# A linear-attention and mixture-of-experts kernel: its large loads on one queue, its gate products on GpSimd, its last batch's P@V in two groups, and a new order of all tasks

## The chip, the core and the metric

The kernel runs on one NeuronCore of a Trainium2 chip. A core has a matrix engine (TensorE, PE in the rows; its weight loads are a row of their own, PEld), a vector engine (VectorE, DVE), a scalar engine (ScalarE, ACT), a general engine (GpSimd, POOL) and an engine that mostly issues transfers (SyncE, SP). Each engine executes its own instructions in the order in which they were written, and waits for the others by semaphores. The core has 16 DMA engines, which move data between the chip's memory and the core's own memory (SBUF). TensorE writes its products to eight PSUM banks, which the other engines read. Transfers are issued by an engine into that engine's queue; here SyncE and ScalarE issue them.

The metric is the device time of one execution in microseconds (us); less is better. A profiled execution gives, beside its time, a trace of each instruction.

## What is computed

There are 8 batches of 8 heads, 576 tokens, head dimension 64. Each head goes through linear attention without a softmax and a root-mean-square norm; the eight heads side by side are the input `x` (8 x 576 x 512) of a layer of four attention experts, of which each token takes two:

```python
kv = np.einsum('bhsd,bhse->bhde', k, v)
out = np.einsum('bhsd,bhde->bhse', q, kv)
x = out / np.sqrt(np.mean(out * out, axis=-1, keepdims=True) + 1e-06) * g_norm
# x: heads side by side, [B, S, 512]
logits = x @ w_gate                      # [B, S, 4]; the two largest are kept
w = softmax over the two kept logits
for e in range(4):                       # head dimension 64, causal
    a = softmax(causal((x @ wq[e]) @ (x @ wk[e]).T / 8))
    ye = a @ (x @ wv[e]) @ wo[e]
    out[tokens that kept e] += w[:, e] * ye
```

## The kernel before, in words

**Tasks.** The whole program is a list of 1071 tasks that the file holds written out; nothing in the file works it out. `names` gives every task its name, `ORDER` holds two base-64 digits for each place in the list, `ENGINE` one letter for each task (S: SyncE's queue, C: ScalarE's queue, A: ScalarE, V: VectorE, G: GpSimd, F: a matmul over all 128 rows where it is over 64 otherwise), and `SLOTS` says which PSUM bank or which buffer each task takes. The loop at the end of the kernel emits the tasks in this order; since every engine executes in order, the list alone sets what stands ahead of what. The semaphores between engines follow from the data.

**A batch** goes through these tasks, in the kernel's names with the lines of the code before:

- `lk`, `lv`: four transfers each for K and V, by half of the heads and by one of two runs of tokens (256 or 320 KB). K and V have two buffers each, and `SLOTS` says which one a batch takes; a load waits until `kv` has read what its buffer held before.
- `lq`: three transfers for Q, one of 576 KB over 128 partitions for the even head pairs and two of 288 KB over 64 partitions for the odd ones. Q has two buffers.
- `kv` (L379): K^T V on TensorE, 80 small matmuls. `kvc`, `kvx`: copies from PSUM to `kvs`, and from there with the 32-row blocks swapped to `kvm` (L392 where GpSimd does it; L296 and L297 are the shared lines of copies on ScalarE and VectorE).
- `qc` (L401): Q is turned on VectorE. `o` (L414): Q times kv on TensorE. `oc`, `sq` (L438 where GpSimd does it): copy and square of the result.
- `ms`, `G` (L446): sums of the squares and the gate's products by matmul; then the inverse root with one step of refinement over three engines (`ln`, `rs`, `na`, `nb`, `lo`, and `R`, L485). `bc` (L521): the inverse root is spread over partitions by matmul; `xm` (L528): the product is `x`, transposed.
- `L`, `lt`, `ltc`, `lgc`, `m8` ... `gate`: the gate's logits, the two largest of four and their weights, on small tiles.
- `v` (L580), `kp`, `qp` (L600): projections by the weights, which are scaled by `g_norm` beforehand (`lw` loads 256 KB, `ws`, L361 on ScalarE, scales); copies `vc`, `kpc`, `qpc`.
- for each of two pairs of experts: `sc` (L630) scores, `exp` (L642) on ScalarE, `msk` (L649) the causal mask on GpSimd, `pv` (L661) P times V, whose 65th column holds the sum of P.
- `rc` (L676): the reciprocal of that sum on VectorE. `iv` (L680): its product with the gate, ten numbers for each of 128 partitions, on GpSimd or VectorE. `oc2` (L688): the scaling of P@V, on VectorE, for both experts of a pair at once. `ot` (L700): the result is turned on TensorE, `otc` copies it.
- `y` (L727): the product with `wo`, `yc` its copy into one of nine stage buffers (which the weights use too at the start), `st` the store to memory. Every second batch has one more `y` for the last 64 rows of two batches.

The tasks of a batch are interleaved with those of the batches beside it; around 167 us, for example, TensorE does projections and scores of one batch, y of the one before and K^T V of the next.

**Zero matmuls.** `ZEROS` puts 69 matmuls of zeros ahead of four TensorE tasks of the first batch (43 before its first K^T V). Their results aren't used. Being float32, each is two passes (L762, 138 rows).

**Queues.** ScalarE's queue has two loads each of K and V of batch 0, all six Q loads of batches 0 and 1, three of the six loads of wq, wk and wv, and two of the last stores. All else is on SyncE's. Each queue is issued in order: where a transfer has to wait for its buffer, all behind it on that queue wait too.

Of the kernel before, what the change touches and what calls it, by code (L numbers as in the profile page):

```python
# [25 lines left out]
    ("kv", 0, 0): 43, ("o", 0, 1): 12, ("ms", 0): 9, ("bc", 0, 0, 1): 5,  # L26
# [3 lines left out]
    "0602040801000703050U0V0A0W092U0X0Y2T0f0C0g0a0b0B0c0e2V0Z0i0d2N0n2L2S2h0o0h2i0q2R0D0k2M0m0p2O0r2Q0j0l2P0t0u2g0s"  # L30
    "0v0w0K0O0x0G132W2f2X150y0z112Y2Z2a2d160M12142c2e170+182b2k0L0-0H2r2j4R2n0E1q0I0N2l2p1o0P2s2q2m4X0F1H1p2o101L1M"
    "194T2t1r1R1N1I4Q1S2u2v2w4V1s2x2y2z4S334a2+2-1O4Y0J374Z1P344U1C1t381T1w1Q354b361A1U1x391V1X301Y3A3T1e313V1W3U1Z"
    "1y4c4n4W4d4k6c4e1a321z1b3W4l1c3X8b4f213b3P4i6Y1B6b1D1J6U4j6S3L3Q8Z4g1E6a3c6V4h1F4m3M3B1K6X4o203Y4q1f6Z6T4s1g4p"
    "3C1G4w6n4u3Z1u1v4r3f3s3t0Q3q6W4v3r8X223E6o3D1h4t1d4x3a3N1i4y1-1j4+8e1+1k4-231l3O8Y24506m3y0S3u6d6e3z513v6f6g3+"
    "3F5258258d6p6h3-8c26AZ428g3d3g6l538h3G1m3e8a5AAb6j5C1n6k6i4z595B3w5D543x5E0R0T5F6q6r3H6u6s273J8f6w285Y5O6v6x3R"
    "Ai6y5a5Z3i6t3h6z5U5V6+3K558u5P3S6-8i8r4470718j8k8lAgAf56725b3j5773745G3I8s5H8m5c757G7H5dAh8nAj763k5J2F8p7C5Q3l"
    "8oAd3m5R7D8q3n5v415w2G5S7A7E8t5k2I7F5T5x2J7BAa5y5I8w915e5g8-8v92908z5f773o5h8+7W5i5KAc8x788y435-3p5j5z6393Av60"
    "5+7940CgAw619545Ae645LAu6962467U5W5o7cCk96975l477X4898Cm7aAt7x99Cn687bAk7I7V5n5X7d7y9FEo9L7L9JAl5M9M9K9G7JAmAn"
    "66Ao7e7i7kArEqAp2CCi5mEm7l9AAs7S65677T5p2D5q7f7j5N5r497z9H7K5s4AEn947+Aq9IAyB3B181CoCj4HAx82Az6A4I4NA-B07Y9V9X"
    "4BB49W4K6BCeCl6CA+9Y9B4C7Q6D7Z7MB2El7g4D4O4L7R7h887-9CB57mB7Cz9DB829A2C+B97NBA9EB6A37pEh6E807q6F7o9N5tBBBH9O9f"  # L40
    "2AEp9g9hBC5uA0BI9iBN9dC-CfBDBO7nA17O9eBJ7PChBK7r7s9p9q839n84CpBEA47t7uA89oCqCyA5878AA9CrCs85Ct9v869j9QCvBLBFA6"
    "Cx6G4ECuCwBM9kA79PD18BBG6HD84FD02KD69R89BPD29l8C8DD9EiE-2H6MBQD48EC46N8F9SEkD7BX9bD3ACD59c9ZDA9mF1AAF07v4PEjEg"
    "BS9aAB8G6P8H7wBYDCDDE+C59T4GDEErEsDFEtDGBR6Q6REu6JEvC29tExC3BjEyBkDSBh9s6K9UDQBZDT9u4MAFBfDRBiDMEwBgBaEz2EBrBs"
    "BTDH9rBlBmDODBDPDNF2F6BxDIF4ADF39wBnFAAE9x9y9zC8F72BAGF8AHC9Bo8O9+AI8UFBAJBbCABU8PDJF9AKF5FC9-CC8VCBC6DKCDFEBp"
    "DmBqBcDnFFC7BdDoFGALFDCFDpBVCG6OBe6LFHBwAMBWDwCEDLFICIDUFOBvDxDq8RFPE7DV8SBtDkDuDrFJFKE8FSFUBuDl6IDvFLFVFTAQCH"
    "CJCKARE9CL4JDgDhCMFMFQEAFRByEHEBEIDyDsECANBzFNB+B-DeDiATDtFWDWFq8TAWAOEJAUFoDcDjD+FkFpFrDdEFDfEDFlAXDXEGD-E0Fw"
    "8LDY8IEL8MFX8JGBGCC0FxDzAPC1EEFmCNFuENEMAVCOFnFsFyFzFt8WCSFiFvFYEK8KDZG1CTFZG9GAFjFeG0F-E1DaGFE2GDFfDbE3E4EO8N"
# [62 lines left out]
def kernel(  # L110
# [690 lines left out]
```

## Time and profile before

| | |
|---|---|
| three runs | 221.35, 223.86, 224.46 us; median 223.86 |
| profiled execution | 223.62 us; span of the trace 221.9 |
| mean granted clock of TensorE | 0.97 |
| first K^T V of batch 0 begins | 13.77 us |
| TensorE's busy share | 92% |
| bytes moved | 40.33 MB, mean 182 GB/s |

The span is the time from the first to the last instruction of the trace, and what the execution takes beyond it is 1.7 us. A row of a timeline gives the start in us, the duration in us, the engine, the line of the code, the operation, the tile written and the tiles read, their shapes, the number of instructions that were drawn together, and in square brackets for how long the engine had been idle before and what ended the idle time. A row of a group gives the busy time in us and the mean duration of one in ns behind the first bar, and the idle time before them by what ended it behind the second. A row of a line gives the least, middle and longest duration in ns, and the stretch of time in which they lie. A row of the transfers gives the size of one in KB and the middle time in us from issue to landing.

### The profile page before, as it was taken

The page shows a single profiled execution, that of the slowest core. Times are in us where ns is not written, and L with a number is a line of the kernel's source. Part 1 is how long each engine was busy: PE and PEld are TensorE (multiplying, and loading weights), DVE is VectorE, ACT ScalarE, POOL GpSimd, SP SyncE. Part 2 cuts the span into 40 slices and gives each one's busy share as a digit, 9 for nine tenths or more (in the row PEclk, how much of TensorE's full clock was granted, in tenths as well). Part 3 has the DMA queues.
Part 4 walks back from the last instruction along what each step waited for, and adds up shares of the span by engine and source line. Part 5 has one row for each costly group of instructions (what it writes and reads, how often), then busy time and mean ns, then how long its engine had stood idle before and what let it go on. Part 6 is the DMA issues. An engine that isn't in the chain of part 4 may idle for free.

```text
span 221.9 us, 7348 instructions
## 1 busy us (share of the span) xinstructions
PE 204.1 (92%) x3082; PEld 170.3 (77%) x3082; DVE 131.5 (59%) x320; ACT 130.4 (59%) x225; POOL 63.4 (29%) x164
## 2 busy tenths in 40 slices
PE   7999798199999899999999999999996999999990
PEld 7987585177877878796897869878965788999970
DVE  6005578018764883997686477468557457454770
ACT  2002802376769674558645886877566585867851
POOL 7001000010157115317340351143357142234300
PEclk9999999769999999999999999999999799999997
DMA  5999999994079999974089369210270001036386
GB/s 177 357 216 296 293 242 315 238 243 85 4 201 352 334 252 268 233 237 159 4 213 268 116 178 358 92 50 0 100 284 3 1 3 47 28 120 233 99 326 246
DMA packets 34385, 40.33 MB, mean 182 GB/s; under 512 B 9008, under 2 KB 25392, under 8 KB 34352
## 3 DMA queue, kind: packets, MB, share of 16 engines
q1 hardware_dynamic: 28736, 34.95, 54.2%
q10 hardware_dynamic: 5616, 4.92, 8.6%
q8 instruction: 24, 0.39, 0.8%
q14 instruction: 9, 0.07, 0.1%
HBM read 30.42 MB, written 9.44 MB: 180 GB/s over the span
## 4 chain that ended last, share of the span: by engine, by line
PE 69%; DMA 17%; DVE 4%; issue 3%; ACT 3%; SPq 1%; ACTq 0%; DVEq 0%
PE banks L600 15%; PE banks L580 8%; PE banks L630 7%; PE banks L379 6%; PE banks L727 6%; PE banks L661 6%; PE banks L762 6%; DMA stage<-in_moe_wq_dram 6%; PE banks L446 5%; PE banks L414 5%; DMA stage<-in_moe_wv_dram 4%; DMA q_b<-in_q_dram 3%; DMA k_b<-in_k_dram 3%; PE banks L521 3%; DMA out_dram<-stage 2%
## 5 line engine op out<-in xcount | busy, mean ns | idle before, releaser
L642 ACT ACTIVATE PT<-banks 128x1024 bf16<-128x1024 f32 (+1 forms) x64 | 51.8, 839 | 12.2 <-PE banks L630 11.5
L649 POOL TENSOR_SCALAR_AFFINE_SELECT PT<-PT 128x256 bf16<-128x256 bf16 (+1 forms) x80 | 29.1, 383 | 28.6 <-ACT PT L642 28.2
L401 DVE STREAM_TRANSPOSE qT<-q_b 128x576 f32<-128x576 f32 x32 | 23.8, 760 | 9.5 <-DMA q_b<-in_q_dram 6.5
L528 DVE TENSOR_TENSOR xT<-banks,ob 128x576 fp32r<-128x576 f32 x32 | 23.3, 752 | 7.8 <-PE banks L521 7.1
L600 PE MATMUL banks<-xT,wq_r 128*128 128x288 f32 x128 | 21.0, 310 | 5.1 <-ACT wq_r L361 5.1
L438 POOL TENSOR_TENSOR sqs<-ob 128x576 f32<-128x576 f32 x15 | 17.1, 1145 | 29.9 <-ACT ob L296 23.1
L580 PE MATMUL banks<-wv_r,xT 128*128 128x256 f32 x160 | 25.4, 296 | 0.0
L727 PE MATMUL banks<-wo_b,OT 128*128 128x256 bf16 x144 | 21.6, 282 | 2.3 <-DVE osc L688 2.1
L600 PEld LDWEIGHTS banks<-xT,wq_r 128*128 128x128 f32 x128 | 18.4, 197 | 6.2 <-ACT wq_r L361 5.4
L379 PE MATMUL banks<-v_b,k_b 128*64 128x64 f32 x640 | 21.6, 224 | 1.1 <-issue 0.7
L580 PEld LDWEIGHTS banks<-wv_r,xT 128*128 128x128 f32 x160 | 22.1, 199 | 0.4 <-issue 0.3
L379 PEld LDWEIGHTS banks<-v_b,k_b 128*64 128x64 f32 x640 | 19.8, 138 | 3.4 <-issue 1.6
L630 PE MATMUL banks<-qTp,kT 64*128 64x192 f32 (+3 forms) x224 | 22.3, 307 | 0.0
L762 PE MATMUL banks<-zeros 128*128 128x128 f32 x138 | 19.3, 307 | 2.2 <-DVE zeros L192 1.1
L762 PEld LDWEIGHTS banks<-zeros 128*128 128x128 f32 x138 | 18.5, 220 | 3.4 <-DVE zeros L192 1.1
L630 PEld LDWEIGHTS banks<-qTp,kT 64*128 64x128 f32 x224 | 15.9, 185 | 6.7 <-issue 1.7
L600 PE MATMUL banks<-xT,wk_r 128*128 128x288 f32 x128 | 20.4, 302 | 0.1
L414 PE MATMUL banks<-qT,kvs 32*64 32x288 f32 x256 | 19.7, 411 | 0.2
L414 PE MATMUL banks<-qT,kvm 32*64 32x288 f32 x256 | 18.9, 411 | 0.0
L296 ACT COPY ob<-banks 128x576 f32<-128x576 f32 x21 | 12.8, 651 | 10.4 <-PE banks L414 10.4
L600 PEld LDWEIGHTS banks<-xT,wk_r 128*128 128x128 f32 x128 | 17.6, 188 | 0.9 <-issue 0.4
L661 PEld LDWEIGHTS <-PT 128*128 128x128 bf16 x480 | 15.6, 97 | 2.8 <-issue 1.2
(95 smaller groups left out, 304.2 us busy)
## 6 DMA issues: line engine op xcount, KB each, us to landing
out_dram<-stage SPq DMA_DIRECT2D x30, 256.0 KB, 2.6
k_b<-in_k_dram SPq DMA_DIRECT2D x15, 320.0 KB, 8.2
v_b<-in_v_dram SPq DMA_DIRECT2D x14, 320.0 KB, 7.0
v_b<-in_v_dram SPq DMA_DIRECT2D x16, 256.0 KB, 7.4
k_b<-in_k_dram SPq DMA_DIRECT2D x15, 256.0 KB, 6.4
q_b<-in_q_dram SPq DMA_DIRECT2D x12, 288.0 KB, 7.7
q_b<-in_q_dram SPq DMA_DIRECT2D x6, 576.0 KB, 7.4
q_b<-in_q_dram ACTq DMA_DIRECT2D x2, 576.0 KB, 5.8
```

The costliest lines, as they stand in the source:

```text
L379: use(nc.tensor.matmul(p_kv[hh * Dh : (hh + 1) * Dh, c, :], lhsT=k_t(b)[:, h, j, :], rhs=v_t(b)[:, h, j, :], start=(j == 0), stop=(j == LO ...
L401: nc.vector.transpose(q_part(b, dh)[:, ms].rearrange("p m (t i) -> p m t i", t=RUN), q_t(b)[:, ms, :, dh * 32 : (dh + 1) * 32],)
L414: use(nc.tensor.matmul(bank(n)[at : at + Dh, 0:HALF], lhsT=(kvs if z == dh else kvm)[b % 2][pp, m], rhs=q_part(b, dh)[pp, m], start=(dh == ...
L528: use(nc.vector.tensor_tensor(out=at_half(xTs[b % 2], u, z), in0=both(ns)[:, :, 0:HALF], in1=ob[:, u::2, z * HALF : (z + 1) * HALF], op=Al ...
L580: use(nc.tensor.matmul(bank(n)[:, 0 : E * Hd], lhsT=blocks_of(xTs[b % 2], c)[:, i * P : (i + 1) * P], rhs=w_r["v"][:, c, :, :].rearrange(" ...
L600: use(nc.tensor.matmul(bank(ns[s])[:, 0:HALF], lhsT=w_r[nm][:, c, 2 * pr : 2 * pr + 2, :].rearrange("p e f -> p (e f)"), rhs=blocks_of(xTs ...
L630: use(nc.tensor.matmul(bank(ns[el])[:, o : o + hi - lo], lhsT=kTs[(2 * b + pr) % 3][pp, kb * P : (kb + 1) * P], rhs=tiles["qTp", b, pr][pp ...
L642: use(nc.scalar.activation(PTs[(2 * b + pr) % 3][:, :, 512 * j : 512 * j + o], both(ns)[:, :, 0:o], ACTF.Exp, scale=scale), *ns)
L649: nc.gpsimd.affine_select(out=d, in_=d, compare_op=AluOpType.is_ge, fill=0.0, base=0, pattern=[[0, 2], [1, w]], channel_multiplier=-1,)
L661: use(nc.tensor.matmul(bank(ns[el])[:, qc * W1 : (qc + 1) * W1], lhsT=PT[:, el, col : col + P], rhs=vexts[b % 2][:, kb, 2 * pr + el, :], s ...
L727: use(nc.tensor.matmul(bank(n)[:, cols], lhsT=OT[:, pr, at : at + P], rhs=wo_b[:, pr, cols], start=(pr == 0), stop=(pr == EP - 1), skip_gr ...
L762: use(nc.tensor.matmul(bank(at)[:, 2 * P : 3 * P], lhsT=zeros[:, 0:P], rhs=zeros[:], start=True, stop=True, skip_group_check=True), at)
```

## The change

- **Loads.** All loads of K, V and of wq, wk, wv, and all stores, are issued by SyncE. Of Q, one of the two transfers of the odd head pairs of batch 0 stays with ScalarE; `lq` is now two tasks, one with one transfer and one with two. The two small loads of `g_norm` and `w_gate` move to ScalarE's queue. SyncE's order at the start is: K and V of batch 0, Q of batch 0, Q, K and V of batch 1, then the first half of wv, the second of wk and both of wq, one V load of batch 2 (into the buffer that batch 1's V has), the second half of wv and the first of wk, and then the rest of batch 2. No wait or counter was written for this: the list of tasks holds it.
- **Engines.** All products with the gate (`iv`) are on GpSimd, 18 of them (before: 6 on GpSimd, 10 on VectorE). GpSimd also gets two more squares, eight more `kvx` copies, three more `R` and one weight scaling, three `mk`, and gives five of seven `lgc` to VectorE. ScalarE gets eight more of the `yc` copies (22 to 30), VectorE has 6 in place of 14. Five of the twelve spread matmuls over 128 rows become ones over 64.
- **The last batch** does `pv`, `rc`, `iv`, `oc2`, `ot` and `otc` in two groups of query blocks, 0 to 2 and 3 to 4, for each pair of experts. In a group both experts share one PSUM bank.
- **Zero matmuls**: 61 in place of 69, ahead of five tasks.
- **Order**: 1075 tasks in a new order, with new slots and ten stage buffers. From batch 2 on TensorE's own order is nearly as it was.

The tables `ORDER`, `ENGINE` and `SLOTS` are replaced as a whole and left out here.

```diff
 ZEROS = {
-    ("kv", 0, 0): 43, ("o", 0, 1): 12, ("ms", 0): 9, ("bc", 0, 0, 1): 5,
+    ("kv", 0, 0): 28, ("kv", 0, 2): 4, ("o", 0, 1): 17, ("ms", 0): 6, ("bc", 0, 0, 0): 6,
 }
...
+def groups_of(b, nb):
+
+    return ((0,), (1,)) if b == nb - 1 else ((),)
...
-        out += [("lq", b, x) for x in range(3)]
+        out += [("lq", b, x) for x in r2]
...
-            out += [(m, b, p) for m in ("pv", "rc", "iv", "oc2")]
-            out += [(m, b, p) for m in (("ot", "otc") if b in BY_PE else ("td", "tl"))]
+            out += [(m, b, p) + g for g in groups_of(b, nb) for m in ("pv", "rc", "iv", "oc2")]
+            out += [(m, b, p) + g for g in groups_of(b, nb) for m in (("ot", "otc") if b in BY_PE else ("td", "tl"))]
...
-    def lq(b, x):
-        pp = slice(0, P) if x == 0 else slice((x - 1) * Dh, x * Dh)
-        dst = q_t(b)[pp, min(x, 1) :: 2].rearrange("i m t d -> i m (t d)")
-        if x == 0:
-            src = q[b].rearrange("(m k a) (i t) d -> k (a i) m (t d)", k=2, a=2, t=RUN)[0]
-        else:
-            src = q[b, head(x - 1, 1) :: 4].rearrange("m (i t) d -> i m (t d)", t=RUN)
-        queue(("lq", b, x)).dma_start(dst, src)
+    def lq(b, odd):
+        eng = nc.scalar if b == 0 else nc.sync
+        if not odd:
+            nc.sync.dma_start(
+                q_t(b)[:, ::2].rearrange("i m t d -> i m (t d)"),
+                q[b].rearrange("(m k a) (i t) d -> k (a i) m (t d)", k=2, a=2, t=RUN)[0],
+            )
+            return
+        for a in range(2):
+            (eng if a else nc.sync).dma_start(
+                q_t(b)[a * Dh : (a + 1) * Dh, 1::2].rearrange("i m t d -> i m (t d)"),
+                q[b, head(a, 1) :: 4].rearrange("m (i t) d -> i m (t d)", t=RUN),
+            )
...
-    def pv(b, pr):
-        ns, PT = big("pv", b, pr), PTs[(2 * b + pr) % 3]
-        for qc in range(NB):
+    def group(g):
+        return range(NB) if not g else range(3) if g[0] == 0 else range(3, NB)
+
+    def pv_at(b, pr, g):
+        qs = group(g)
+        if not g:
+            ns = big("pv", b, pr)
+            return ns, [bank(n)[:, 0 : NB * W1] for n in ns], both(ns)[:, :, 0 : NB * W1].rearrange(
+                "p e (n f) -> p e n f", f=W1)
+        ns, w = small("pv", b, pr, *g), len(qs) * W1
+        t = bank(ns[0])[:, 0 : 2 * w]
+        return ns * 2, [t[:, 0:w], t[:, w:]], t.rearrange("p (e n f) -> p e n f", e=2, f=W1)
+
+    def pv(b, pr, *g):
+        PT = PTs[(2 * b + pr) % 3]
+        ns, heads, _ = pv_at(b, pr, g)
+        for k_, qc in enumerate(group(g)):
...
-                        bank(ns[el])[:, qc * W1 : (qc + 1) * W1],
+                        heads[el][:, k_ * W1 : (k_ + 1) * W1],
...
-    def ot_copy(b, pr):
-        (n,) = small("ot", b, pr)
-        use(copy(("otc", b, pr), OT[:, pr, b % 2 * S : (b % 2 + 1) * S], bank(n).bitcast(BF16)[:, 0:S]), n)
+    def ot_copy(b, pr, *g):
+        (n,) = small("ot", b, pr, *g)
+        spans = {(): ((0, S),), (0,): ((REM, REM + 3 * P),), (1,): ((0, REM), (REM + 3 * P, S))}[g]
+        for lo_, hi_ in spans:
+            at = b % 2 * S
+            use(copy(("otc", b, pr) + g, OT[:, pr, at + lo_ : at + hi_], bank(n).bitcast(BF16)[:, lo_:hi_]), n)
```

The functions `rc`, `ivm`, `o_scale` and `ot` take the group in the same way: they work on its query blocks alone.

More of the change, by code (lines that the diff above doesn't have):

```diff
@@ L33 @@
[L33 to L47, printed above, removed]
@@ L667, in pv, with inv_of @@
                     ), ns[el])
-    def heads_out(b, pr):
-        ns = big("pv", b, pr)
-        return ns, both(ns)[:, :, 0 : NB * W1].rearrange("p e (n f) -> p e n f", f=W1)
-    def rc(b, pr):
-        ns, po = heads_out(b, pr)
-        iv = buf(("inv", b, pr), [P, 2, NB], FP32, "inv")
-        use(nc.vector.reciprocal(iv[:].unsqueeze(3), po[:, :, :, Hd : Hd + 1]), *ns)
-    def ivm(b, pr):
-        iv = tiles["inv", b, pr][:]
-        ew(("iv", b, pr)).tensor_tensor(
-            out=iv, in0=iv, in1=tiles["gate", b][:, :, 2 * pr : 2 * pr + 2].rearrange("p n e -> p e n"),
+    def inv_of(b, pr, g):
+        qs = group(g)
+        return buf(("inv", b, pr), [P, 2, NB], FP32, "inv")[:, :, qs[0] : qs[-1] + 1]
@@ L682, in ivm, with rc, osc_of @@
+    def rc(b, pr, *g):
+        ns, _, po = pv_at(b, pr, g)
+        use(nc.vector.reciprocal(inv_of(b, pr, g).unsqueeze(3), po[:, :, :, Hd : Hd + 1]), *ns)
+    def ivm(b, pr, *g):
+        iv, qs = inv_of(b, pr, g), group(g)
+        ew(("iv", b, pr) + g).tensor_tensor(
+            out=iv, in0=iv, in1=tiles["gate", b][:, qs[0] : qs[-1] + 1, 2 * pr : 2 * pr + 2].rearrange("p n e -> p e n"),
             op=AluOpType.mult,
         )
-    def o_scale(b, pr):
-        ns, po = heads_out(b, pr)
-        osc = buf(("osc", b, pr), [P, NB, 2, Hd], BF16, "osc")
+    def osc_of(b, pr, g):
+        return buf(("osc", b, pr), [P, NB, 2, Hd], BF16, "osc")
@@ L688, in o_scale @@
+    def o_scale(b, pr, *g):
+        (ns, _, po), qs = pv_at(b, pr, g), group(g)
         use(nc.vector.tensor_tensor(
-            out=osc[:].rearrange("p n e f -> p e n f"),
+            out=osc_of(b, pr, g)[:, qs[0] : qs[-1] + 1].rearrange("p n e f -> p e n f"),
             in0=po[:, :, :, 0:Hd],
-            in1=tiles["inv", b, pr][:].unsqueeze(3).to_broadcast([P, 2, NB, Hd]),
+            in1=inv_of(b, pr, g).unsqueeze(3).to_broadcast([P, 2, len(qs), Hd]),
             op=AluOpType.mult,
@@ L693, in o_scale, with ot_at, ot @@
         ), *ns)
-    def ot(b, pr):
-        (n,) = small("ot", b, pr)
+    def ot_at(b, qc):
+        return (0 if qc == NF else REM + qc * P) if b % 2 else qc * P
+    def ot(b, pr, *g):
+        (n,) = small("ot", b, pr, *g)
         p_t = bank(n).bitcast(BF16)
-        for qc in ((NF,) if b % 2 else ()) + tuple(range(NF)) + (() if b % 2 else (NF,)):
-            at = (0 if qc == NF else REM + qc * P) if b % 2 else qc * P
+        for qc in sorted(group(g), key=lambda qc: ot_at(b, qc)):
+            at = ot_at(b, qc)
```

59 lines of the change are left out of this document (37 added, 22 removed).

## The prediction

> **What bounds the kernel now.** I read the page's first two parts, then the stretches by window, then who waits for whom.
>
> ```profile
> PE 204.1 (92%) x3082; PEld 170.3 (77%) x3082; DVE 131.5 (59%) x320; ACT 130.4 (59%) x225; POOL 63.4 (29%) x164
> ...
> PE   7999798199999899999999999999996999999990
> ...
> PEclk9999999769999999999999999999999799999997
> ```
>
> TensorE (PE) is busy 92% of the span, and the other engines 59% at most: TensorE bounds the kernel. The question is therefore only where its row is below 9, or PEclk is low, and what the change does there. Three places show: slices 7 and 8, counted from 0 (39 to 50 us: PE 1, then PEclk 7 and 6), slice 30 (166 to 172 us: PE 6) and the end.
>
> ```profile
> 36.86 1.32 PE L600 MATMUL banks<-xT,wk_r 128*128 128x288 f32 x8
> 43.31 2.29 PE L600 MATMUL banks<-xT,wq_r 128*128 128x288 f32 x8 [5.13 <-ACT wq_r L361]
> ```
> ```profile
> ACT wq_r L361 <- DMA stage<-in_moe_wq_dram: 8.0, 1, 8.0
> ```
> ```profile
> 36.90:43.30 6.40, 1.28 (x11) 1.04 (x8) 2.21 (x4) 0.77 (x2) 0.00 (x0) 0.84 1.07 272
> 43.30:49.00 5.70, 5.69 (x34) 4.49 (x35) 1.10 (x6) 4.14 (x9) 1.52 (x3) 0.58 1.08 246
> ```
>
> The first place: the first K projection of batch 0 runs at 36.86, the first Q projection only at 43.31. TensorE idles 5.13 us, because ScalarE (ACT) waits 8.0 us for the wq weights. The rows of stretches give us, busy time of PE, PEld, DVE, ACT and POOL, granted clock, DMA share and GB/s. In the 5.70 us after the wait the clock is 0.58, so that the same eight matmuls take 2.29 us and not 1.32. During the wait the DMA engines are full (share 1.07) and move 272 GB/s: they carry other bytes than the ones that are waited for.
>
> ```profile
> k_b<-in_k_dram SPq DMA_DIRECT2D x15, 320.0 KB, 8.2
> ...
> k_b<-in_k_dram SPq DMA_DIRECT2D x15, 256.0 KB, 6.4
> q_b<-in_q_dram SPq DMA_DIRECT2D x12, 288.0 KB, 7.7
> q_b<-in_q_dram SPq DMA_DIRECT2D x6, 576.0 KB, 7.4
> ...
> stage<-in_moe_wq_dram SPq DMA_DIRECT2D x1, 256.0 KB, 7.2
> ...
> stage<-in_moe_wq_dram ACTq DMA_DIRECT2D x1, 256.0 KB, 12.5
> ```
>
> The two halves of wq are equal in size. The one on SyncE's queue landed 7.2 us after its issue, the one on ScalarE's queue 12.5 us. By the order of issue, SyncE was then loading batch 2's k and v beside it.
>
> **The change part by part.** The profiled execution took 223.62 us (span 221.9, 1.7 outside it); the median shown is 223.86, so the sum on the profiled one stands for the median within 0.3.
>
> *1. Loads on one queue, weights before batch 2.* In the new order SyncE issues batch 0, batch 1, then wv, wk, wq, wq, one load of v for batch 2, wv, wk, and then the rest of batch 2. Of the large loads only half of the odd heads' q of batch 0 stays with ScalarE.
>
> ```profile
> 2.40:14.00 11.60, 11.60 (x89) 11.48 (x90) 2.55 (x16) 0.00 (x0) 2.41 (x10) 1.00 1.06 307
> 14.00:26.00 12.00, 10.78 (x202) 8.76 (x198) 4.72 (x8) 5.02 (x10) 0.78 (x2) 1.00 1.07 279
> 26.00:42.50 16.50, 11.14 (x202) 8.23 (x202) 10.70 (x23) 2.92 (x6) 0.39 (x1) 0.96 1.18 274
> 42.50:52.00 9.50, 8.69 (x66) 6.63 (x66) 2.87 (x10) 7.28 (x14) 1.52 (x3) 0.71 1.04 221
> ```
>
> A batch is k 2 x 320 + 2 x 256 KB, v as much, q 1152 KB: 3456 KB, 3.54 MB. By 26.0 us the old loads had moved 307 x 11.6 + 279 x 12.0 = 6.91 MB. At these rates the new order has batches 0 and 1 (7.08 MB) at 26.6 us, the first four weights (1.05 MB) at 30.4, the two others (with 0.33 MB of v between) at 33.5, and the rest of batch 2's k and v (2.03 MB) at 41.
>
> ```profile
> 29.77 1.39 PE L379 MATMUL banks<-v_b,k_b 128*64 128x64 f32 x40
> ```
>
> The one load of v before the last two weights waits for the first half of batch 1's K^T V, whose buffer it takes, and both weights stand behind it on SyncE. That half would end at 29.8 + 1.4 - 2.1 (step 2) = 29.1, while the queue still holds weights until 30.4: no gap. The first Q projection can follow the K projection at once, and the 5.13 us go. Next late is wv for the first value block, some 3 us after that projection begins: with the lead of step 2 at about 39, so 5 us to spare. **-5.1**. With the idle time goes the slow clock after it: 0.42 x 5.70 = 2.4 us; I take **-2.0**, because a restart without any gap isn't shown.
>
> *2. Fewer zero matmuls.* The table falls from 69 to 61 calls, 138 to 122 passes.
>
> ```profile
> L762 PE MATMUL banks<-zeros 128*128 128x128 f32 x138 | 19.3, 307 | 2.2 <-DVE zeros L192 1.1 <-ACT sqs L434 0.6 <-DVE kvs L297 0.5
> ```
> ```profile
> 28.11 0.52 DVE L479 SCALAR_TENSOR_TENSOR lo<-root,low,hi 128x288 fp32r<-128x288 f32 x1
> ```
> ```profile
> 28.13 1.38 PE L762 MATMUL banks<-zeros 128*128 128x128 f32 x10
> 29.44 0.40 PE L521 MATMUL banks<-lo,spread 64*128 64x288 f32 x2
> ```
>
> These fill TensorE until data come, and now and then run too long: the last ten end at 29.5 and hold the spread matmuls, whose input was ready at 28.63. A pass is 19.3 / 138 = 0.14 us, 16 fewer are 2.2. The bounds are 0 (data set the pace) and 3.5 (data earlier still); I take **-2.1**.
>
> *3. Gate products (L680), and more, on GpSimd.*
>
> ```profile
> 167.81 2.25 POOL L438 TENSOR_TENSOR sqs<-ob 128x576 f32<-128x576 f32 x2
> ```
> ```profile
> 167.95 2.50 DVE L680 TENSOR_TENSOR inv<-inv,gate 128x10 f32<-128x10 f32 x1
> ```
> ```profile
> 171.37 1.04 PE L727 MATMUL banks<-wo_b,OT 128*128 128x256 bf16 x4 [2.09 <-DVE osc L688]
> ```
> ```profile
> L680 DVE TENSOR_TENSOR inv<-inv,gate x10: 176/177/2497, 118.1 to 211.7; 128x10 f32<-128x10 f32 x10
> L680 POOL TENSOR_TENSOR inv<-inv,gate x6: 213/214/215, 71.6 to 149.9; 128x10 f32<-128x10 f32 x6
> ```
>
> This is slice 30. A product of ten numbers, 177 ns in the median, took 2497 on VectorE (DVE), as long as two GpSimd squares ran beside it, and TensorE waited 2.09 us. On GpSimd the product stands in that engine's own row and holds no VectorE instruction that long: **-2.1**. [...]
>
> Against it stands the hop through GpSimd between reciprocal and scaling:
>
> ```profile
> L688 DVE TENSOR_TENSOR osc<-banks,inv 128x640 bf16<-128x640 f32 x16 | 13.1, 820 | 1.2 <-POOL inv L680 0.8
> ```
> ```profile
> L438 POOL TENSOR_TENSOR sqs<-ob 128x576 f32<-128x576 f32 x15 | 17.1, 1145 | 29.9 <-ACT ob L296 23.1 <-DVE ob L297 6.8
> L392 POOL COPY kvm<-kvs 32x256 f32<-32x256 f32 x11 | 4.5, 411 | 43.9 <-ACT kvs L296 24.4 <-DVE kvs L297 19.2
> L485 POOL TENSOR_TENSOR rstd<-hi,lo 128x288 f32<-128x288 f32 x3 | 2.4, 802 | 0.0
> ...
> L680 POOL TENSOR_TENSOR inv<-inv,gate 128x10 f32<-128x10 f32 x6 | 1.3, 214 | 7.8 <-DVE inv L676 7.8
> ```
>
> Six such hops cost VectorE 0.8 us of waiting; 18 would cost 2.4. GpSimd gets 12 products (2.6), 8 kvm copies (3.3), 2 squares (2.3), 3 rstd (2.4), 3 masks and one weight scaling (2 at most, from the 1145 of a square), and gives 5 logit copies away: some 75 us, a third of the span. A product that finds a square ahead of it in the queue comes 1.1 us late, and the scaling and all behind it on VectorE with it. Bounds 0 and 18 x 1.1 = 20; I take **+2.5** for the hops and for small waits of the new order, near the six that are shown.
>
> *4. P@V of the last batch in two groups; copies dealt anew.* The same matmuls, four more small VectorE and two more GpSimd instructions; y copies on ScalarE go from 22 to 30.
>
> ```profile
> 210.00:217.40 7.40, 6.20 (x80) 4.87 (x78) 4.62 (x11) 4.49 (x8) 0.00 (x0) 1.00 0.88 320
> ```
> ```profile
> 213.64 1.81 ACT L296 COPY stage<-banks 128x512 f32<-128x512 f32 x3 [0.69 <-DMA out_dram<-stage]
> ```
>
> From 210 to the last matmuls TensorE idles 1.2 us, which is what better cover can give there; a copy waits 0.69 for a store. The last chain (product, scaling, turn, copy, two y tiles, stores) stays. **-0.5**, between -1.9 and +1 (two more hops). A tenth stage buffer, five full-width spread matmuls fewer and all stores on SyncE cost nothing that the rows show.
>
> **Sum:** -5.1 - 2.0 - 2.1 - 2.1 + 2.5 - 0.5 = -9.3; 223.6 - 9.3 = 214.3, **214 us**.
>
> **The rivals.**
>
> *One queue is too slow (same).* For it speaks the 221 GB/s of 42.5 to 52, when SyncE alone fed q and the rest; against it, the following row, SyncE alone as well, for 39 us:
>
> ```profile
> 61.00:100.00 39.00, 37.82 (x679) 31.30 (x676) 27.76 (x66) 25.64 (x48) 14.85 (x36) 1.00 0.96 267
> ```
> ```profile
> 55.09 0.73 PE banks L379 x20
> ```
>
> At 221 from the start the 11.0 MB up to batch 2's k and v are in at 2.4 + 49.8 = 52.2. They are wanted where batch 2's K^T V stands: 55.09 less 7.2 of lead and 2.4 of slow clock, 45.5. TensorE waits up to 6.7: 221 us. [...] No run here has the same loads on one queue yet.
>
> *GpSimd becomes the gate (slower).* The place is the moved product; the price is that of slice 30, 2.1 us of TensorE, where the product waits behind squares or masks. It decides from 7 of the 18 pairs: 214 + 7 x 2.1 = 228.7, over 2% slower. With 8 of them 231. Against it: in the kernel before, GpSimd stood ready for its products and waited 7.8 us for VectorE's reciprocals; the other way round the wait was 0.8 in all.
>
> *Nothing new waits.* Without the +2.5: 211.5; with all clock loss and a better end, 209 to 210.
>
> **How the numbers follow.** The forecast's own case (210 to 218) gets 0.64, the slow queue 0.16, GpSimd's gate 0.11, the better case 0.09. A measurement of this kernel, whose three runs spread over 1.4%, tells about 2% from no change: faster is under 219.4, slower over 228.3. A third of the slow queue's case lies under 219.4: faster 0.64 + 0.09 + 0.05 = 0.78; slower 0.10 of GpSimd's 0.11; same 0.12. The range is 209 to 222: it takes in the slow queue and the better case, and leaves out GpSimd's gate and the rims.
>
> **What would show it.** In the new profile wq's copy waits under 1 us for its DMA, the first Q projection begins at 35 to 37 us, and PEclk has no 6 or 7 before slice 10. No L680 row shows VectorE; slice 30 is 9. Idle of VectorE put down to GpSimd's products stays under 3 us. I am wrong if TensorE waits for k, v or wk between 35 and 50 us (slow queue), or if the scaling waits for GpSimd by more than 10 us in all.

## The result, and the profile after

The changed kernel takes 210.15 us (median of 4 runs, 209.54 to 210.51); the kernel before took 222.71 beside it. The ratio is 0.9429, 95% interval 0.9344 to 0.9514: faster by 12.6 us, where 9.3 were forecast. The profiled executions stand 13.4 us apart in their spans (221.9 and 208.5).

The first two parts of the page of the changed kernel:

```profile
PE 195.4 (94%) x3066; PEld 163.2 (78%) x3066; DVE 123.3 (59%) x305; ACT 129.6 (62%) x229; POOL 73.7 (35%) x185
...
PE   7779879999999999999999999999999999999990
...
PEclk9999999999999999999999999999999999999997
```

The holes of before are gone: slices 7 and 8, slice 30, and the 6 and 7s of PEclk. One more of these 7s was in the quoted row of before, in slice 31, and the prediction passed over it. New is a poorer start: the first six digits are 777987 in place of 799979.

The timeline of the changed kernel where the first hole was (start and duration in us):

```profile
37.44 1.32 PE L610 MATMUL banks<-xT,wk_r 128*128 128x288 f32 x8
38.60 1.22 PE L610 MATMUL banks<-xT,wq_r 128*128 128x288 f32 x8
```

The first Q projection follows the first K projection at once, at full clock (1.22 us against 2.29). The two halves of wq came in by the row of the transfers of the changed kernel

```profile
stage<-in_moe_wq_dram SPq DMA_DIRECT2D x2, 256.0 KB, 5.5
```

in 5.5 us, and SyncE, with one load of 288 KB left on ScalarE's queue, moved as much as the two queues together had. The stretches of the prediction, of the changed kernel (us, busy time of PE, PEld, DVE, ACT, POOL, clock, DMA share, GB/s):

```profile
2.40:14.00 11.60, 9.13 (x100) 8.68 (x99) 2.94 (x15) 0.00 (x0) 1.73 (x10) 1.00 1.01 273
14.00:26.00 12.00, 10.16 (x170) 8.47 (x174) 6.03 (x13) 3.90 (x7) 0.90 (x2) 1.00 1.07 320
```

By 26 us that is 273 x 11.6 + 320 x 12.0 = 7.0 MB; before it was 6.9. What TensorE waits for longest now (us in total, times, longest):

```profile
PE banks L389 <- DMA v_b<-in_v_dram: 2.9, 2, 2.0
PE banks L793 <- DVE root L484: 1.2, 1, 1.2
...
```

These, and the two next (1.1 and 0.9 us ahead of zero matmuls), lie in the first batch, and the first row is new: K^T V of batch 0 waits for V, where zeros ran before.

**Where the 13.4 us went.** TensorE's busy time fell by 204.1 - 195.4 = 8.7; its idle time, with the end behind it, by the other 4.7.

| | us | from |
|---|---|---|
| wait for wq | -5.1 | waits before |
| wait for the scaling in slice 30 | -2.1 | waits before |
| half clock behind these two waits | -3.9 | 0.42 x 5.70 = 2.4, and 1.5 in slice 31 (below) |
| zeros | -2.9 | 19.3 to 16.4 by the groups |
| wait for V of batch 0 | +2.9 | waits after |
| other busy time of TensorE | -1.9 | 8.7 - 3.9 - 2.9 |
| end behind the last matmul | -0.4 | 221.9 - 216.4 = 5.5 and 208.5 - 203.4 = 5.1 |
| all other waits | 0 | 4.7 less the three waits and the end |

A part of the other busy time is the five full-width spread matmuls that became half-width ones: the groups of that line were 5.2 and 6.5 us before, and are

```profile
L531 PE MATMUL banks<-lo,spread 64*128 64x288 f32 x50 | 7.4, 334 | 0.0
...
L531 PE MATMUL banks<-lo,spread 128*128 128x288 f32 x14 | 3.1, 300 | 0.0
```

10.5 after: 1.2 us less.

### The profile page after: what moved, and what is told of

It reads as the page before. It is cut to its first block, busy times and chain, and to the rows that moved or that the text cites. A ratio compares the mean times of both kernels' runs of the same rounds, so it can differ in the third digit from the quotient of the medians.

```text
span 208.5 us, 7342 instructions
## 1 busy us (share of the span) xinstructions
PE 195.4 (94%) x3066; PEld 163.2 (78%) x3066; DVE 123.3 (59%) x305; ACT 129.6 (62%) x229; POOL 73.7 (35%) x185
## 4 chain that ended last, share of the span: by engine, by line
PE 83%; DMA 8%; ACT 4%; DVE 2%; issue 1%; SPq 0%; POOL 0%; ACTq 0%; DVEq 0%; POOLq 0%
PE banks L610 17%; PE banks L590 9%; PE banks L389 9%; PE banks L424 8%; PE banks L640 8%; PE banks L456 8%; PE banks L685 7%; PE banks L758 6%; PE banks L793 3%; PE banks L531 3%; DMA v_b<-in_v_dram 3%; DMA k_b<-in_k_dram 3%; PE banks L728 2%; DMA out_dram<-stage 2%; ACT stage L301 1%; PE banks L514 1%
## 5 line engine op out<-in xcount | busy, mean ns | idle before, releaser
L652 ACT ACTIVATE PT<-banks 128x1024 bf16<-128x1024 f32 (+1 forms) x64 | 51.0, 838 | 11.8 <-PE banks L640 10.4
L448 POOL TENSOR_TENSOR sqs<-ob 128x576 f32<-128x576 f32 x17 | 19.4, 1146 | 16.0 <-ACT ob L301 15.4
L590 PEld LDWEIGHTS banks<-wv_r,xT 128*128 128x128 f32 x160 | 21.1, 189 | 1.1 <-issue 0.5
L758 PE MATMUL banks<-wo_b,OT 128*128 128x256 bf16 x144 | 20.4, 274 | 0.0
L610 PE MATMUL banks<-xT,wq_r 128*128 128x288 f32 x128 | 20.3, 300 | 0.0
L793 PE MATMUL banks<-zeros 128*128 128x128 f32 x122 | 16.4, 296 | 3.8 <-DVE root L484 1.2
L610 PE MATMUL banks<-xT,wk_r 128*128 128x288 f32 x128 | 19.7, 298 | 0.0
L793 PEld LDWEIGHTS banks<-zeros 128*128 128x128 f32 x122 | 15.4, 208 | 5.0 <-DVE root L484 1.7
L301 ACT COPY stage<-banks 128x512 f32<-128x512 f32 x30 | 17.2, 594 | 2.9 <-PE banks L758 1.7
L402 POOL COPY kvm<-kvs 32x256 f32<-32x256 f32 x19 | 7.6, 398 | 29.8 <-ACT kvs L301 16.2
```

The source lines that it names most:

```text
L301: return nc.scalar.copy(dst, src)
L590: use(nc.tensor.matmul(bank(n)[:, 0 : E * Hd], lhsT=blocks_of(xTs[b % 2], c)[:, i * P : (i + 1) * P], rhs=w_r["v"][:, c, :, :].rearrange(" ...
L610: use(nc.tensor.matmul(bank(ns[s])[:, 0:HALF], lhsT=w_r[nm][:, c, 2 * pr : 2 * pr + 2, :].rearrange("p e f -> p (e f)"), rhs=blocks_of(xTs ...
L652: use(nc.scalar.activation(PTs[(2 * b + pr) % 3][:, :, 512 * j : 512 * j + o], both(ns)[:, :, 0:o], ACTF.Exp, scale=scale), *ns)
L758: use(nc.tensor.matmul(bank(n)[:, cols], lhsT=OT[:, pr, at : at + P], rhs=wo_b[:, pr, cols], start=(pr == 0), stop=(pr == EP - 1), skip_gr ...
L793: use(nc.tensor.matmul(bank(at)[:, 2 * P : 3 * P], lhsT=zeros[:, 0:P], rhs=zeros[:], start=True, stop=True, skip_group_check=True), at)
```

## The experiments

All of them were timed beside the kernel before on the same chip. Its median was 221.1 to 222.4 there; its executions there spread from 219.8 to 224.1, and the profiled one (223.6) is near the upper end. In code, `lw` is the load of a weight, and a letter is the task's place in `ENGINE`.

### One load moved

```diff
-("lw", "q", 1): "C"    # ScalarE's queue
+("lw", "q", 1): "S"    # SyncE's queue
```

> The kernel before with one load moved: the half of wq that was on ScalarE's queue is issued by SyncE, at its place in the list. Theory A (the wait and the slow clock behind it are all there is): the 5.1 us of TensorE's wait and the 2.5 us of half clock behind it go, 223 - 7.6 = 215.4. Theory B (the bytes set the pace: 256 KB more ahead of batch 2 make K and V of batch 2 late): TensorE waits for batch 2 instead, and 2 us or less are gained, 221 or more. Theory C (the order of all loads is needed for the gain, one load is not enough): wk or wv is late next, 2 to 5 us gained, 218 to 221.

Measured: 215.69 us against 221.51, ratio 0.9707 (0.9636 to 0.9778). From the timeline of this kernel:

```profile
36.45 1.33 PE L600 MATMUL banks<-xT,wk_r 128*128 128x288 f32 x8
37.62 1.22 PE L600 MATMUL banks<-xT,wq_r 128*128 128x288 f32 x8
```

Theory A holds: one letter takes wait and slow clock away, nothing is late in its place, and all later batches run 7.9 to 8.3 us earlier than in the profile of before. The medians give 5.8 and not 7.6. In another execution with the old loads, that of the kernel with one product on GpSimd (below), the wait and the clock behind it were

```profile
PE banks L600 <- ACT wq_r L361: 4.2, 1, 4.2
```
```profile
42.70:46.20 3.50, 3.06 (x13) 3.06 (x14) 0.74 (x2) 3.25 (x6) 1.29 (x2) 0.51 1.08 230
```

4.2 + 0.49 x 3.06 = 5.7: the stall varies from one execution to the next.

### The weights issued earlier by ScalarE

```diff
 lv(1, 1, 1)                                   # ScalarE's queue
+lw(k, 1), lw(v, 1), lw(q, 1)                  # ScalarE's queue
 sq(0, ...), oc(0, ...), ln, rs, na of batch 0 # ScalarE
-lw(k, 1), lw(v, 1), lw(q, 1)
```

> The kernel before with the three weight loads of ScalarE's queue left on that queue, but issued ahead of ScalarE's squares and norm of batch 0 rather than behind them. If it was the late issue that made wq late (it was issued at 29.96 us), wq lands 7 to 8 us after an issue at 22 to 25 us, at 30 to 33. If sharing with SyncE's loads on a second queue made it slow, it takes 12 us again and lands at 34 to 37. TensorE wants it at 38: in both cases the wait goes and the time is about 215.4 (223 - 7.6). If the loads of batch 1 lose by it what wq gains, K^T V of batch 1 starts later than 29.8 us and less is gained.

Measured: 224.25 us, ratio 1.0098 (1.0057 to 1.0138): slower, which no theory had. The waits of TensorE and of ScalarE, and from the timeline the last of the three issues and the squares behind it:

```profile
PE banks L762 <- ACT sqs L434: 7.6, 1, 7.6
```
```profile
ACT sqs L434 <- DMA v_b<-in_v_dram: 7.1, 1, 7.1
```
```profile
24.87 3.03 ACTq L352 DMA_DIRECT2D stage<-in_moe_wq_dram  x1
27.95 2.28 ACT L434 ACTIVATE sqs<-banks 128x576 f32<-128x576 f32 x4 [7.12 <-DMA v_b<-in_v_dram]
```

ScalarE issued the three loads at 22.62, 23.62 and 24.87 us, and the last issue itself took 3.03 us. Its squares of batch 0, next in its order, began at 27.95 us, 7.12 us after its work before them, an idle time that the trace puts down to an earlier load, of V; TensorE stood behind the squares for 7.6 us. The wait for wq was gone, and this one had taken its place. wq itself landed 10.8 us after its issue, at 35.6 us, nearer to the 12 expected of a slow second queue than to the 7 to 8 of a late issue; the two before it on that queue took 7.9 and 9.1.

### Another of the three weights last

```diff
-lw(k, 1), lw(v, 1), lw(q, 1)    # order on ScalarE's queue
+lw(q, 1), lw(k, 1), lw(v, 1)
```

> The kernel before with the three weight loads of ScalarE's queue in another order: wq, wk, wv in place of wk, wv, wq; queue and places stay. Theory A (the last of the three is slow, because it is issued as SyncE begins batch 2's loads, whichever it is): wq lands 6 to 7 us after its issue, at 33 to 34, and wv takes 11 to 13 us and lands at 41 to 43; the first Q projection no longer waits, but the first value block waits in its place, and 1 to 3 us are gained, 218.5 to 220.5. Theory B (it is wq itself, or its buffer): wq lands late again and the time is 221.5. Theory C (chance of one execution): all three land in 5 to 8 us, and 6 to 7 us are gained.

Measured: 221.05 us, ratio 0.9964 (0.9919 to 1.0009). The transfers on ScalarE's queue, with the time from issue to landing, and what TensorE waits for:

```profile
stage<-in_moe_wq_dram ACTq DMA_DIRECT2D x1, 256.0 KB, 5.4
stage<-in_moe_wk_dram ACTq DMA_DIRECT2D x1, 256.0 KB, 7.2
stage<-in_moe_wv_dram ACTq DMA_DIRECT2D x1, 256.0 KB, 13.2
```
```profile
PE banks L580 <- ACT wv_r L361: 4.6, 1, 4.6
```

Theory A, but for the gain, which isn't clear of noise: the third is slow whichever it is, and the wait only changes its name. It was issued at 29.26 us, as SyncE began batch 2. ScalarE's queue as such isn't slow (5.4 and 7.2 us for the first two); the third place is, beside the next batch's loads. Whether these loads make it slow or the two loads ahead of it was not tried apart.

### One gate product on GpSimd

```diff
-("iv", 4, 0): "V"
+("iv", 4, 0): "G"
```

> The kernel before with one gate product of ten numbers, that of the first pair of experts of batch 4 (2.50 us on VectorE beside two squares), on GpSimd at its place in the list, ahead of these squares. Theory A (wait and slow clock): 2.1 us of TensorE's wait and 1.7 us of half clock behind it go, 223 - 3.8 = 219.2. As the prediction had it (wait alone): 220.9. Rival (the product is held on GpSimd instead, behind a square of 1.1 us, or VectorE's wait for it takes its place): 222 to 223.

Measured: 220.07 us, ratio 0.9890 (0.9807 to 0.9973). In its timeline:

```profile
166.39 0.22 POOL L680 TENSOR_TENSOR inv<-inv,gate 128x10 f32<-128x10 f32 x1 [3.84 <-DVE inv L676]
...
167.93 2.25 POOL L438 TENSOR_TENSOR sqs<-ob 128x576 f32<-128x576 f32 x2
...
168.78 1.78 DVE L680 TENSOR_TENSOR inv<-inv,gate 128x10 f32<-128x10 f32 x1
```

The moved product takes 0.22 us ahead of the squares; the next product, still on VectorE, is held for 1.78 in its stead, until the squares have ended. From y of batch 3 on the lead over the profile of before is 2.1 us greater than ahead of it. No half clock followed, but TensorE has two waits of 0.6 us there. The time lies between theory A and the prediction's figure.

### Both edits

```diff
-("lw", "q", 1): "C", ("iv", 4, 0): "V"
+("lw", "q", 1): "S", ("iv", 4, 0): "G"
```

> The kernel before with both edits: wq's half on SyncE's queue and the one gate product on GpSimd. Theory A: the two stalls are independent, 223 - 7.6 - 3.8 = 211.6, within 1.5 us of the changed kernel (210.2), so that all the rest of the change is worth 1 to 2 us. If the new order of the rest is needed: 214 or more.

Measured: 214.30 us, ratio 0.9659 (0.9593 to 0.9725), 7.2 us less than before: the two gains (5.8 and 1.4) add up. Two letters of the tables bring some 60% of the 12 us. Theory A was 2.7 us too low. The second held product and the spread of before (above) are likely reasons; this run doesn't separate them.

### All ten products on GpSimd, and the load

```diff
-("lw", "q", 1): "C", ("iv", b, p): "V"   # ten of the sixteen
+("lw", "q", 1): "S", ("iv", b, p): "G"
```

> The kernel before with wq's half on SyncE's queue and all ten gate products of VectorE on GpSimd, at their places in the list. With only the first product of batch 4 moved the next one was held in its place (1.78 us on VectorE), and the time was 214.3. Theory A (the held product is the rest of that stall): another 1.0 to 1.8 us go, 212.5 to 213.3. If the other products lose by the hop as the prediction's step 3 allowed (0.14 us each at the six that were shown, up to 1.1 behind a square): 214.3 to 216. If TensorE's order has work enough for either: 214.3.

Measured: 213.26 us, ratio 0.9648 (0.9598 to 0.9697). From its timeline, the pair of batch 4:

```profile
161.72 0.22 POOL L680 TENSOR_TENSOR inv<-inv,gate 128x10 f32<-128x10 f32 x1 [3.85 <-DVE inv L676]
...
164.35 0.21 POOL L680 TENSOR_TENSOR inv<-inv,gate 128x10 f32<-128x10 f32 x1
```

Neither is held now, and over this stretch the kernel gains 1.0 us on the one with both edits: theory A at its lower end. In the last 20 us of these two executions it loses 0.6; whether that is the hops was not separated. By medians the gain is 1.0, with intervals that overlap. The profiled execution (215.09 us) is the slowest of its four: TensorE waits 2.1 us for the scaled `w_gate` there, from 25.9 us on, with half clock behind it from 28.4 to 31.8 us, far ahead of this stretch.

### The changed kernel again, and with all products on VectorE

```diff
-("iv", b, p): "G"    # all 18
+("iv", b, p): "V"
```

> The changed kernel once more, as the measure for the three others of this call: 210.0, within 0.7 us.

> The changed kernel with all 18 gate products on VectorE at their places in the list. Theory A (the engine is what counts: on VectorE one of them is held beside a GpSimd square again): one row of over 1 us among them, and 1 to 4 us slower, 211 to 214. Theory B (the new order counts: after the P@V of batch 4 TensorE has a value block, scores and sums of squares to do, so that a late product holds nothing): within 0.7 us of 210, whether or not a product is held; the 4.0 us that VectorE waits for GpSimd's products in the changed kernel are worth nothing either.

Measured: 209.99 us (ratio 0.9478, 0.9416 to 0.9540) and 209.82 (0.9474, 0.9395 to 0.9553). The line of the products on VectorE, and one of them beside a square, in the second kernel:

```profile
L703 DVE TENSOR_TENSOR inv<-inv,gate x18: 133/176/1846, 61.1 to 200.3; 128x10 f32<-128x10 f32 x14, 128x6 f32<-128x6 f32 x2, 128x4 f32<-128x4 f32 x2
```
```profile
95.74 1.14 POOL L448 TENSOR_TENSOR sqs<-ob 128x576 f32<-128x576 f32 x1
...
97.34 1.85 DVE L703 TENSOR_TENSOR inv<-inv,gate 128x10 f32<-128x10 f32 x1
98.01 1.14 POOL L448 TENSOR_TENSOR sqs<-ob 128x576 f32<-128x576 f32 x1
```
```profile
159.41 0.17 DVE L703 TENSOR_TENSOR inv<-inv,gate 128x10 f32<-128x10 f32 x1
```

Theory B. A product, the second of batch 1, is held for 1.85 us, and nothing comes of it; its scaling stands at 100.64 us, behind other work of VectorE, and no wait of TensorE follows. The first product of batch 4, which was held before, takes 0.17 us here (last row): in the new order it isn't held on VectorE either. So the new order has taken that product away from the squares, and it has room for the one that is held; this run doesn't tell what a held product of batch 4 would cost in it. The 4.0 us of VectorE's waits for GpSimd are worth next to nothing: without them the last matmul ends at 202.8 us, against 203.2 in the changed kernel again, and 0.3 us of that were there ahead of the first product (61 us).

### The zero matmuls

Two kernels, the first with the counts of before, the second with fewer:

```diff
-("kv", 0, 0): 28, ("kv", 0, 2): 4, ("o", 0, 1): 17, ("ms", 0): 6, ("bc", 0, 0, 0): 6
+("kv", 0, 0): 43,                  ("o", 0, 1): 12, ("ms", 0): 9, ("bc", 0, 0, 0): 5
```
```diff
-("kv", 0, 0): 28, ("kv", 0, 2): 4, ("o", 0, 1): 17, ("ms", 0): 6, ("bc", 0, 0, 0): 6
+("kv", 0, 0): 28, ("kv", 0, 2): 4, ("o", 0, 1): 14, ("ms", 0): 4, ("bc", 0, 0, 0): 2
```

> The changed kernel with the counts of zero matmuls of before (43 ahead of the first K^T V, none ahead of its third part, 12, 9, 5). As the prediction's step 2 had it (16 passes fewer save 2.1 us): 210 + 2.1 = 212.1. Theory A (data and the engines behind them set the pace of the first batch, the zeros only fill; the first spread matmul of batch 0 began at 29.4 before and 29.8 after): 0 to 0.7 us slower.

> The changed kernel with fewer zeros where they end after the data that they wait for: 14 in place of 17 ahead of the first Q times kv, 4 in place of 6 ahead of the sums of squares, 2 in place of 6 ahead of the first spread matmul, which they hold until 29.9 us although its input is ready at 28.8. Theory A (only what lies between ready data and the end of the zeros is to be had): 0.5 to 1.1 us faster than the changed kernel, 209 to 209.5. If every pass counted (18 passes of 0.14 us): 2.5 us faster. If a later wait (wk, K^T V of batch 1) takes the lead away: no difference.

Measured: 210.78 us (ratio 0.9511, 0.9448 to 0.9573) and 210.07 (0.9438, 0.9344 to 0.9532), beside 209.99. With the old counts:

```profile
13.72 2.55 PE L389 MATMUL banks<-v_b,k_b 128*64 128x64 f32 x80
...
29.67 0.53 PE L531 MATMUL banks<-lo,spread 64*128 64x288 f32 x4
```

K^T V of batch 0 begins 3.0 us later and runs in one piece, and the first spread matmul begins at 29.67, against 29.65 in the changed kernel again: no difference. What it is longer comes from 118 us on, where no zeros are. With the trimmed counts the first spread matmul and all behind it came 0.7 us earlier, as theory A had it, but the span was no shorter: 5.9 us lay between the last matmul and the end, against 4.9. TensorE waited 2.1 us for V at its start, and PEclk has a 6 in slice 2 (10.4 to 15.6 us). So 16 passes fewer are worth nothing, and those that outlast their data 0.7 us at the last matmul, which the time doesn't show.

### The last batch in one piece

```diff
 def groups_of(b, nb):
-    return ((0,), (1,)) if b == nb - 1 else ((),)
+    return ((),)
...
+# pv, rc, iv, oc2, ot, otc of batch 7 at the places of their second groups; y, yc, st of batch 7 behind them
```

> The changed kernel with the last batch's P@V, reciprocals, products, scalings, turns and copies in one piece for each pair of experts, at the places that the second groups have, and its y tiles behind both turns. The prediction's step 4 gave the groups 0.5 us, between 1.9 gained and 1 lost. Theory A (the groups let y of the first three blocks run under the second group's chain): TensorE waits 1 to 2 us for the last scaling and turn, and the time is 1 to 2 us longer, 211 to 212. If the last chain hides behind other work anyway: 210.

Measured: 212.92 us, ratio 0.9619 (0.9579 to 0.9659), 2.9 slower than the changed kernel. New among TensorE's waits, and by stretch:

```profile
PE banks L728 <- DVE osc L713: 1.3, 2, 1.0
...
PE banks L758 <- ACT OT L301: 1.1, 2, 0.7
```
```profile
196.00:199.90 3.90, 3.68 (x76) 3.45 (x76) 0.62 (x3) 2.45 (x6) 0.86 (x3) 1.00 0.97 329
199.90:203.30 3.40, 1.34 (x16) 0.92 (x15) 1.63 (x3) 1.28 (x2) 0.21 (x1) 1.00 0.43 161
203.30:206.80 3.50, 3.50 (x19) 2.15 (x16) 0.69 (x1) 1.70 (x3) 0.00 (x0) 0.51 0.40 152
```

2.4 us of waits, a little over theory A's 1 to 2, and 0.49 x 3.5 = 1.7 of half clock behind them, which it had not. This says what the groups are worth in the new order, not against the old one. There other work covered the tail, as these stretches up to the last matmul show, of the kernel before and of the changed one:

```profile
210.00:216.40 6.40, 6.20 (x80) 4.87 (x78) 4.62 (x11) 3.57 (x7) 0.00 (x0) 1.00 0.86 310
```
```profile
197.00:203.40 6.40, 6.23 (x92) 5.08 (x88) 3.65 (x11) 4.80 (x13) 1.42 (x6) 1.00 0.88 314
```

TensorE is idle for 0.2 us in each.

### A version with better placed zeros

```diff
-("kv", 0, 0): 28, ("kv", 0, 2): 4, ("o", 0, 1): 17, ("ms", 0): 6, ("bc", 0, 0, 0): 6
+("kv", 0, 0): 34, ("kv", 0, 2): 6, ("o", 0, 1): 14, ("ms", 0): 4, ("bc", 0, 0, 0): 2
```

> The changed kernel with fewer zeros behind K^T V of batch 0 (14, 4 and 2 for 17, 6 and 6) as in the run with trimmed zeros, and more ahead of and within K^T V of batch 0 (34 and 6 for 28 and 4), so that TensorE has no wait of 2 us there. Theory: the last matmul ends 0.7 us earlier than in the changed kernel, as with the trimmed zeros, and no stretch of half clock appears at 11 us; time 209.3. If the end is set by the stores: 210.

Measured: 208.51 us, median of 6 runs, ratio 0.9419 (0.9371 to 0.9468): the lowest median of all. The last matmul ends at 202.5 us, against 203.2, and the wait for V is 0.5 us in place of 1.6. The interval overlaps that of the changed kernel, so the 0.8 us of the trace are shown and the difference in time isn't.

## Why the prediction was right, step by step

The forecast was 214 us, and 210 came: sign, main cause and range held. On the profiled executions 9.3 us were forecast and 13.4 came: the zeros were 2.1 too good, the hops 2.5, the slow clock 1.9 and TensorE's other work 1.9 too bad, the end 0.1 too good. That the sum came so near is in part luck: the zeros (-2.1) and the hops (+2.5) both measured 0 and cancelled each other.

*Step 1, the wait for wq: -5.1, and it was that; one moved load reproduces it alone.* Nothing was late in its place: wv, named as next, lands in time. The half clock was put at -2.0 for want of a row without a gap; it was all of the 2.4. The comparison of the two halves of wq was too simple. The transfers of before have these rows too:

```profile
stage<-in_moe_wk_dram ACTq DMA_DIRECT2D x1, 256.0 KB, 6.1
stage<-in_moe_wv_dram ACTq DMA_DIRECT2D x1, 256.0 KB, 6.6
```

Two of the three loads on ScalarE's queue were no slower than SyncE's; only the last, which met batch 2, took 12.5. The queues of before from 37.0 us to 42.5, when wq landed (q1 is SyncE's, q10 ScalarE's; packets, MB, share of 16 engines):

```profile
q1 hardware_dynamic: 1001, 1.51, 103.6%
q10 hardware_dynamic: 137, 0.03, 3.4%
```

The last 137 of wq's 1024 packets of 256 bytes were what took so long, beside 1.51 MB of batch 2. What holds them back within the DMA engines was not separated.

*Step 2, the zeros: -2.1, measured 0.* The step took the last ten zeros, which do outlast their data, as the price of all. The others filled time until data came, and what was taken away there came back as a wait for V (-2.9 and +2.9). The lead that step 1 drew on didn't come either: the first Q projection begins at 38.60 us, not at 35 to 37, though right behind the K projection. The bound "0 (data set the pace)" was the right end.

*Step 3, the held product: -2.1, measured -3.6.* The wait went as forecast, but the 1.5 us of half clock behind it were missed, though PEclk's row showed them. And the cause of the gain was only half right: on GpSimd the product is short, as forecast (0.22 us), yet the new order alone does as much, since with all products back on VectorE the time is the same (209.82 us against 209.99). What holds a product on VectorE beside GpSimd's squares isn't shown; rows of such products have 2.50, 1.78 and 1.85 us. The 3.6 are read from the traces; in the old order, the runs with the products moved gave 1.4 for the first and 1.0 for the others, by medians.

*Step 3, the hops: +2.5, measured 0.* VectorE did wait, 4.0 us where the prediction said to stay under 3 (the first row, of its waits; the second is of GpSimd's):

```profile
DVE osc L713 <- POOL inv L703: 4.0, 9, 0.7
```
```profile
POOL inv L703 <- DVE inv L699: 22.2, 12, 5.6
```

TensorE's waits have no row that comes from it. VectorE, busy for 59% of the span, had room for these 4.0 us; the term was worked out on VectorE and charged to TensorE, which was the error.

*Step 4, the end: -0.5, measured -0.4,* all of it behind the last matmul (5.5 us to 5.1). In the other runs of the changed order with the groups this stretch is 4.8 to 5.9 us long, so the 0.4 isn't clear of the spread. The 1.2 us of idle time that the step read as room lay there too, but for 0.2. The groups hold this end in the new order (2.9 us without them). The spread matmuls, put at nothing, were 1.2 us in TensorE's busy time; the row that shows it, line 521 by shapes, wasn't read.

*The rivals.* One slow queue: refuted, with 7.0 MB by 26 us. GpSimd as the gate: refuted; GpSimd waited 22.2 us for VectorE's reciprocals, and VectorE 4.0 for the products. Nothing new waits (209 to 211.5, chance 0.09): this is what came but for the wait for V, and it was given too little.

About 3 us of the gain belong to the rest of the change: with the load and all products moved, the kernel before comes to 213.26, and the changed one is at 210. The spread matmuls are 1.2 us of TensorE's busy time. What the rest comes from stays open: only the zeros, the groups and the products' engine were tried, and these in the new order alone.

## What to carry to other kernels

Price a stall of TensorE by the wait and by the slow clock that may follow it (here 5.1 us and 2.4 behind them, 2.1 and 1.5), and read the clock's row in every slice before the sum. Charge a wait to the path only if something on the bounding engine stops for it: a product held for 2.50 us cost 2.1 us and more in one order, and another held for 1.85 us nothing in the other. And load what is needed first ahead of the next batch (one such load was worth 5.8 us), on an engine whose own work isn't queued behind the issue (where ScalarE's squares were, TensorE waited 7.6 us).

## What the runs showed of the hardware

In these traces the half clock ahead of the last matmul came in pieces of one length, 3.4 us. By windows of the kernel before (the seventh column is the granted clock):

```profile
41.20:44.60 3.40, 1.29 (x5) 1.29 (x6) 0.00 (x0) 2.07 (x4) 0.66 (x1) 0.51 1.06 254
44.60:48.10 3.50, 3.50 (x21) 2.81 (x23) 1.10 (x6) 2.29 (x5) 0.85 (x3) 0.50 1.07 238
```
```profile
167.50:170.90 3.40, 1.78 (x41) 1.50 (x38) 3.13 (x3) 2.44 (x3) 2.92 (x5) 1.00 0.02 5
170.90:174.40 3.50, 3.03 (x17) 2.56 (x17) 2.38 (x7) 1.27 (x2) 0.00 (x0) 0.51 0.00 0
```

In both places the clock is 1.00 again behind these rows. At 170.9 us half clock lasted one piece, at 41.2 two. In the first of the two TensorE was busy for 1.29 of 3.40, and in the kernel with wq first on ScalarE's queue for 2.56 of 3.50, with half clock again behind it, up to 49.2 us:

```profile
42.30:45.80 3.50, 2.56 (x16) 2.06 (x20) 0.00 (x0) 2.89 (x6) 0.00 (x0) 0.50 0.94 202
```

By windows of 0.01 us the clock of the kernel before falls at 41.26 us, is whole again at 48.08, falls at 170.96, is whole at 174.37, and falls at 218.75, behind the last matmul. These stretches of 6.82, 122.88, 3.41 and 44.38 us, those at whole clock too, are 2, 36, 1 and 13 times 3.413 us. In the execution with all ten products on GpSimd the clock falls at 28.41 and at 212.73 us, 54 such pieces apart. That the other executions keep this step is an estimate from these two.

Waits of one length had two prices. 2.09 us at 169.28 cost 3.03 x 0.49 = 1.5 more. In the kernel with wq first the same matmuls wait 2.08 us for the same scaling, from 167.4 to 169.4 us. There, by this estimate, the border of two pieces (37 of them behind 42.3, at 168.6) falls into the wait; neither piece is as empty as the one with 1.78 us above, and the clock stays whole:

```profile
165.20:168.60 3.40, 2.16 (x54) 1.85 (x50) 2.76 (x3) 2.82 (x4) 3.29 (x5) 1.00 0.02 5
168.60:172.00 3.40, 2.56 (x41) 2.19 (x45) 3.15 (x7) 1.53 (x3) 0.00 (x0) 1.00 0.01 2
```

Behind this wait that kernel's lead over the profile of before is 1.4 us greater than ahead of it, about the price of the half clock. And 2.01 us in the changed kernel cost no more than themselves:

```profile
7.60:11.10 3.50, 1.49 (x16) 1.30 (x14) 0.00 (x0) 0.00 (x0) 0.00 (x0) 1.00 1.11 334
11.10:14.50 3.40, 2.54 (x51) 2.31 (x53) 0.00 (x0) 0.00 (x0) 0.00 (x0) 1.00 1.06 264
```

In the kernel before TensorE was busy for 1.78 of the 3.40 us ahead of the fall at 170.96. In the changed kernel it was busy for 1.49 of 3.50, if the pieces are counted back from 205.5 us, where its clock falls behind the last matmul, and the clock stayed at 1.00; what decides between the two stays open.

One issue of a load held ScalarE for long: in the trace with the weights issued earlier, that of wq took 3.03 us, for 256 KB in runs of 256 bytes; one of V, 320 KB in runs of 1280 bytes, took

```profile
20.25 0.62 ACTq L312 DMA_DIRECT2D v_b<-in_v_dram  x1
```

0.62. The two others of the weights took 0.37 and 0.38, so it isn't their size alone; what the long one waited for isn't shown.
